# Attention with two feed-forward layers on one core: reads in narrower array tiles, and a new order of steps around the layernorm

## The chip, the cores and the metric

The kernel runs on one core of one Trainium2 chip. The metric is the device time of one execution in microseconds, given as the median of the runs.

## The reference, cut to what matters

```python
# x: [8 batches, 8 heads, 512 tokens, 64], state: [8, 8, 32 states, 64], float32
a  = softmax(x @ state.T / 8)          # each token over the 32 states
xread = a @ state                      # what a token reads from the states
a2 = softmax(state @ x.T / 8)          # each state over the 512 tokens
sread = a2 @ x                         # what a state reads from the tokens
x = concat(xread, sread)               # [8, 544, 512], heads side by side
xn = (x - mean) / sqrt(var + 1e-6) * g_ln
x = x + relu(xn @ w_ch1) @ w_ch2       # hidden width 2048
h = relu(x @ w_in); conv = 3-tap convolution of h along the tokens
out = (h * sigmoid(conv)) @ w_out
```

Everything is float32. Most products are split into a high and a low part and done as three faster products (high by high, low by high, high by low), the lines 633 to 635.

## The kernel before, in words

The first feed-forward layer goes in **units**: unit u is the 512 tokens of batch u, and a tail unit takes the 256 state rows of all batches together. They run in the order 1 to 6, tail, 7; unit 0 is part of the start. A unit has 16 hidden chunks m. `L1` makes a chunk (six matmuls of 512 columns), `L2` adds it to four accumulators (twelve). In `L1` the weights are not multiplied with the tokens: `z_tiles` first multiplies the states of the batch with the weights ("Z"), and `L1` multiplies Z with the softmax weights of the tokens (the tiles `AH`, `AL`).

TensorE takes its instructions in program order. Between its products, in a **gap** before and one after each `L2`, the loop at the end of the program calls `gap(m)`, which issues either a Z product (`z_step`) or the next step of a generator, `tasks`. A `yield` is thus a place where one `L1` or one `L2` goes between two steps. The tasks of unit u are `token_norm(u)`, the layernorm factor of its own tokens, and then `attend(u + 1)`, the attention of the next batch for two groups of four heads, g = 0 and 1. In unit 6 `attend(7)` and `tail_norm` follow, and that unit has an additional gap wherever m is not a multiple of three.

`lnorm` sums over the four chunks on VectorE, splits the sum, and sums over the partitions with a matmul with ones (`mean`, line 494); the second such mean gives the variance. `inv_std` makes the factor: Ln and Exp on ScalarE (lines 532 and 533), then four operations on VectorE. `attn` transposes the tokens on VectorE (`xT`, line 383), and then has these steps: `scores` (line 287), `state_weights` (the states' softmax), `token_weights_1`, `state_weights_t` (transposes on TensorE, line 304, copied by ScalarE, line 306), `token_weights_2`, `state_read` (line 314) with `state_scale` and `token_weights_3`, `state_store` (line 339), `token_read` (line 375). The tiles bP, bQ, bR, bU and bV have one buffer each, so that a writer waits for the last reader.

In `token_read` a state tile `s[:, 2 * g + ql]` holds two heads' states in 64 of its 128 rows, and zeros in the others. In `state_read` each product makes 64 states by two heads, of which `state_scale` keeps the half that belongs together:

```python
T.matmul(sr[64 * ql : 64 * ql + 64, :P], E2T[:, ck, 64 * ql : 64 * ql + 64],
         xn4[:, 2 * ql : 2 * ql + 2, ck, :], start=ck == 0, stop=ck == 3)
```

The start, up to some 150 us, is ordered by the string `START`, in which each letter calls the next step of a stream: T is `attend(1)`, P the products of unit 0, b a step of the weights' conversion on VectorE and GpSimd.

Of the kernel before, what the change touches and what calls it, by code (L numbers as in the profile page):

```python
# [42 lines left out]
def kernel(  # L43
# [223 lines left out]
    def prep_state(b):  # L267
        V.transpose(new_sbd(b).rearrange("p q m -> p (q m)"), s_in.rearrange("p q h r -> p (q h r)"))
        state_parts(b)
# [39 lines left out]
    def state_read(b, g, E2T):  # L309
        sr = bank()  # L310
        xn4 = xnt[b, g]
        for ck in range(4):
            for ql in range(2):
                T.matmul(
                    sr[64 * ql : 64 * ql + 64, :P],
                    E2T[:, ck, 64 * ql : 64 * ql + 64],
                    xn4[:, 2 * ql : 2 * ql + 2, ck, :],
                    start=ck == 0,
                    stop=ck == 3,
                )  # L320
        return sr

    def state_scale(g, sr, z2, B):
# [7 lines left out]
            sr[:, :P].rearrange("p (a d) -> p a d", a=2),  # L331
# [37 lines left out]
    def token_read(b, g):  # L369
# [9 lines left out]
    def attn(b, g):  # L379

        B = work
        xT = new(B["Q"], [2, S])
        V.transpose(flat(xT), xin[b, g])
        if (b, g) not in xnt:
            load_xnat(b, g, new("bP", [1024]))
        yield
        yield
        if g == 0:
            yield
        sc = banks["held"] = scores(b, g, xT)  # L390
# [4 lines left out]
        V.transpose(flat(sT), sc)  # L395
        banks["held"] = None
        yield
# [3 lines left out]
        yield  # L401
        aT = new(B["R"], [S])
        token_weights_2(sT, m1, aT)
# [7 lines left out]
        token_weights_3(aT, b, g, slice(0, S))  # L411
        yield
        state_store(b, g, srz)
        yield
        token_read(b, g)
# [59 lines left out]
    def lnorm(X, t, n, B, add, y):  # L475
# [51 lines left out]
        inv_std(mean(), y, new(B["V"], [n]))  # L527
        banks["held"] = None

    def inv_std(var, y, w):  # L530

        A.activation(w, var, AF.Ln, bias=eps)
        A.activation(y, w, AF.Exp, scale=-0.5)
        V.tensor_tensor(w, y, y, op=ALU.mult)
# [3 lines left out]

    def tail_norm_end():

        y = rstd[NB].unsqueeze(1).to_broadcast([P, KC, TAIL])
        t = new("AH0", [KC, TAIL])
        V.tensor_tensor(t, tns[NB], y, op=ALU.mult)
        tns[NB] = t
# [6 lines left out]
    def attend(u):  # L551
        new_xt(u)
        new_parts(u)
        prep_state(u)
# [4 lines left out]
    def token_norm(u):  # L559
        rstd[u] = new(f"rs{u % 2}", [S])  # L560
        yield from lnorm(XT[u], new("tn", [KC, S]), S, work, V, rstd[u])

    def tail_norm():

        tns[NB] = new("tn", [KC, TAIL])
        rstd[NB] = new("bU", [TAIL])
        yield from lnorm(XTt, tns[NB], TAIL, work, V, rstd[NB])
# [598 lines left out]
```

## Time and profile before

| | us |
|---|---|
| median of 3 runs | 1155.05 (1153.73 to 1155.33) |
| profiled execution, its own time | 1156.01 |
| its span, first to last instruction | 1154.2 |
| TensorE busy | 1120.0 |
| VectorE busy | 720.0 |
| ScalarE busy | 440.9 |
| GpSimd busy | 181.7 |

The profile names tiles without their numbers: `pat` are the two PSUM banks of the tasks, `ph` and `acc` those of `L1` and `L2`. A float32 product that is not split shows as two matmul instructions. A matmul's duration in the profile contains the time to fill and empty the array; the distance between two starts is what it costs in a row of them.

### The profile page before, as it was taken

To read this page: it belongs to the slowest core of one execution; us is meant where nothing else is said; L and a number is where in the kernel's file an instruction comes from. 1 tells how busy PE (TensorE), PEld (TensorE's weight loads), DVE (VectorE), ACT (ScalarE), POOL (GpSimd) and SP (SyncE) were. 2 spreads that over 40 slices of the span, in tenths; PEclk is the share of its full clock that TensorE was granted. 3 is DMA by queue.
4 is the path that set the end of the run, shared out by engine and by line. 5 is a ranking of instruction groups with operands and counts; after the bars stand their busy time and mean duration, and the time that the engine had idled before them with its cause. 6 is when DMAs were issued, how large, how long until landed. Compare 5 with 4: busy or idle time off the path is not lost. (4 is left out here: it accounts for less than half of the span.)

```text
span 1154.2 us, 14521 instructions
## 1 busy us (share of the span) xinstructions
PE 1120.0 (97%) x5393; PEld 847.0 (73%) x5393; DVE 720.0 (62%) x1134; ACT 440.9 (38%) x788; POOL 181.7 (16%) x298
## 2 busy tenths in 40 slices
PE   6999999999999999999999999999999999999997
PEld 5544457777777777777767898788788888888885
DVE  5888666665475565664665723577677666666663
ACT  4565334332333233233333212465344334334342
POOL 2433200000000000000000000265433312212210
PEclk7999999999999999999989999999999999999999
DMA  8565262342333233323323124322112102100001
GB/s 283 159 203 165 60 237 91 80 126 72 76 113 93 68 119 110 96 62 103 97 71 94 70 77 164 110 74 92 37 55 73 37 37 82 38 37 37 1 37 45
DMA packets 129282, 106.29 MB, mean 92 GB/s; under 512 B 103332, under 2 KB 107452, under 8 KB 128188
## 3 DMA queue, kind: packets, MB, share of 16 engines
q1 hardware_dynamic: 129212, 105.37, 29.2%
q8 instruction: 42, 0.69, 0.2%
q14 instruction: 28, 0.23, 0.1%
HBM read 83.85 MB, written 21.50 MB: 91 GB/s over the span
## 5 line engine op out<-in xcount | busy, mean ns | idle before, releaser
L653 DVE SCALAR_TENSOR_TENSOR hL<-ph,hH 128x512 fp32r<-128x512 f32 (+1 forms) x128 | 83.4, 655 | 169.9 <-ACT hH L652 169.7
L633 PE MATMUL acc<-hH,w 128*128 128x512 f32 (+1 forms) x480 | 188.2, 392 | 0.0
L635 PE MATMUL acc<-hH,w 128*128 128x512 f32 (+1 forms) x480 | 181.0, 377 | 0.0
L634 PE MATMUL acc<-hL,w 128*128 128x512 f32 (+1 forms) x480 | 180.6, 376 | 0.0
L652 ACT ACTIVATE hH<-ph 128x512 fp32r<-128x512 f32 (+1 forms) x128 | 72.6, 567 | 193.0 <-PE ph L635 155.5
L1079 DVE SCALAR_TENSOR_TENSOR w<-w,cw,w 128x544 f32<-128x544 f32 x128 | 109.8, 859 | 33.4 <-POOL w L1077 31.6
L633 PEld LDWEIGHTS acc<-hH,w 128*128 128x128 f32 x480 | 90.3, 188 | 43.9 <-issue 16.1
L633 PE MATMUL ph<-AH,ZH 128*128 128x512 f32 x256 | 106.3, 415 | 1.5 <-ACT ZH L608 1.5
L635 PEld LDWEIGHTS acc<-hH,w 128*128 128x128 f32 x480 | 90.2, 188 | 17.3
L634 PEld LDWEIGHTS acc<-hL,w 128*128 128x128 f32 x480 | 90.4, 188 | 16.0 <-DVE hL L653 0.3
L635 PE MATMUL ph<-AH,ZL 128*128 128x512 f32 x256 | 100.9, 394 | 0.0
L634 PE MATMUL ph<-AL,ZH 128*128 128x512 f32 x256 | 100.4, 392 | 0.0
L1060 ACT ACTIVATE w<-w 128x544 f32<-128x544 f32 x64 | 42.1, 658 | 142.1 <-DVE w L1079 142.1
L221 POOL TENSOR_TENSOR ctmp<-ctmp,AH 128x512 int32<-128x512 int32 x1 | 1.3, 1300 | 586.4 <-DVE ctmp L220 586.4
L1067 DVE TENSOR_TENSOR w<-w,w 128x512 fp32r<-128x512 f32 x64 | 50.0, 781 | 42.9 <-ACT w L1066 42.2
L1061 DVE TENSOR_TENSOR w<-w,w 128x544 f32<-128x544 f32 x64 | 48.6, 759 | 40.7 <-ACT w L1060 40.7
L633 PEld LDWEIGHTS ph<-AH,ZH 128*128 128x128 f32 x256 | 48.5, 189 | 22.3 <-issue 8.8
L1066 ACT ACTIVATE w<-w 128x512 fp32r<-128x512 f32 x64 | 40.4, 632 | 51.9 <-DVE w L1061 49.7
L635 PEld LDWEIGHTS ph<-AH,ZL 128*128 128x128 f32 x256 | 48.3, 189 | 12.4 <-DVE ZL L609 2.0
L1077 POOL TENSOR_SCALAR w<-w,cw 128x544 f32<-128x544 f32 x64 | 47.8, 747 | 50.1 <-ACT w L1073 46.9
L634 PEld LDWEIGHTS ph<-AL,ZH 128*128 128x128 f32 x256 | 48.5, 189 | 9.7 <-issue 1.2
L676 PE MATMUL acc<-hH,w 128*128 128x512 f32 x112 | 50.4, 594 | 0.0
(465 smaller groups left out, 2252.9 us busy)
## 6 DMA issues: line engine op xcount, KB each, us to landing
r<-w1d SPq DMA_DIRECT2D x64, 512.0 KB, 4.8
r<-in_moe_w_ch_dram SPq DMA_DIRECT2D x16, 512.0 KB, 5.7
w<-in_moe_w_ch_dram SPq DMA_DIRECT2D x16, 512.0 KB, 8.4
x2d<-XT SPq DMA_DIRECT2D x8, 1024.0 KB, 4.9
bP<-in_x_dram SPq DMA_DIRECT2D x112, 64.0 KB, 2.3
bP<-in_x_dram SPq DMA_DIRECT2D x28, 256.0 KB, 3.3
out_dram<-w SPq DMA_DIRECT2D x24, 256.0 KB, 2.2
w1d<-r SPq DMA_DIRECT2D x8, 512.0 KB, 4.8
```

The source lines that it names most:

```text
L633: T.matmul(o, lh, rh, start=first, stop=False)
L634: T.matmul(o, lh, rl, start=False, stop=False)
L635: T.matmul(o, ll, rh, start=False, stop=last)
L652: A.activation(h, p, AF.Relu)
L653: V.scalar_tensor_tensor(l, p, 0.0, f32(h), op0=ALU.max, op1=ALU.subtract)
L676: T.matmul(acc[d], whole2[m][:, c], h, start=m == 0, stop=m == M1 - 1)
L1060: A.activation(c, c, AF.Sigmoid)
L1061: V.tensor_tensor(c, c, h[:, 1 : SEQ + 1], op=ALU.mult)
L1066: A.activation(g[:, 0], c[:, :S], AF.Copy)
L1067: V.tensor_tensor(g[:, 1], c[:, :S], f32(g[:, 0]), op=ALU.subtract)
L1077: G.tensor_scalar(c, h[:, 0:SEQ], cw[:, f : f + 1], 0.0, op0=ALU.mult, op1=ALU.add)
L1079: V.scalar_tensor_tensor(c, h[:, k : k + SEQ], cw[:, k * FF + f : k * FF + f + 1], c, op0=ALU.mult, op1=ALU.add,)
```

## The change

`token_read` passes only the 64 rows that hold states, so that the two products of a pair use different halves of the array's rows. `state_read` makes each head's 32 states alone: 32 weight columns and 64 streamed columns, sixteen products in place of eight; `state_scale` reads that narrower result twice. The tokens' and states' transposes of the next batch (`begin`) are issued between ScalarE's part of the layernorm factor and VectorE's, in the step of the second mean, and the second group's (`tokens_in`) with `token_weights_3`. The second mean of units 1 to 7 comes one step later (`late`). `state_read` comes before `token_weights_2`, one step after `state_weights_t`. Unit 6 no longer has its extra gaps; from m = 6 on every other `L2` is cut in two with a gap in between. The tail's `tns` is no longer multiplied with its factor before `L1`: three steps of `tail_norm` stay in unit 6, the others go to the tail unit with the layernorm of batch 7, every second gap, and `residual` multiplies the accumulators.

```diff
+    def tokens_in(b, g):
+        xts[b, g] = new(work["Q"], [2, S])
+        V.transpose(flat(xts[b, g]), xin[b, g])
+        if (b, g) not in xnt:
+            load_xnat(b, g, new("bP", [1024]))
+
+    def begin(b):
+        new_xt(b)
+        new_parts(b)
         V.transpose(new_sbd(b).rearrange("p q m -> p (q m)"), s_in.rearrange("p q h r -> p (q h r)"))
-        state_parts(b)
+        tokens_in(b, 0)
...
             for ql in range(2):
-                T.matmul(
-                    sr[64 * ql : 64 * ql + 64, :P],
-                    E2T[:, ck, 64 * ql : 64 * ql + 64],
-                    xn4[:, 2 * ql : 2 * ql + 2, ck, :],
-                    start=ck == 0,
-                    stop=ck == 3,
-                )
+                for hh in range(2):
+                    r = slice(64 * ql + 32 * (hh ^ g), 64 * ql + 32 * (hh ^ g) + 32)
+                    T.matmul(
+                        sr[r, :D], E2T[:, ck, r], xn4[:, 2 * ql + hh, ck, :],
+                        start=ck == 0, stop=ck == 3,
+                    )
...
-                T.matmul(xr[ql], s[:, 2 * g + ql], a, start=i == 0, stop=i == 2)
+                r = slice(64 * ql, 64 * ql + 64)
+                T.matmul(xr[ql], s[r, 2 * g + ql], a[r], start=i == 0, stop=i == 2)
...
     def attn(b, g):
...
-        xT = new(B["Q"], [2, S])
-        V.transpose(flat(xT), xin[b, g])
-        if (b, g) not in xnt:
-            load_xnat(b, g, new("bP", [1024]))
-        yield
-        yield
-        if g == 0:
-            yield
-        sc = banks["held"] = scores(b, g, xT)
+        yield
+        if b == 1:
+            yield
+            if g == 0:
+                yield
+        sc = banks["held"] = scores(b, g, xts[b, g])
         yield
...
         V.transpose(flat(sT), sc)
+        yield
         banks["held"] = None
-        yield
         token_weights_1(sT, m1)
         yield
         E2T = state_weights_t(E2, B)
-        yield
-        aT = new(B["R"], [S])
-        token_weights_2(sT, m1, aT)
         yield
         sr = state_read(b, g, E2T)
...
         srz = state_scale(g, sr, z2, B)
+        yield
+        state_store(b, g, srz)
+        aT = new(B["R"], [S])
+        token_weights_2(sT, m1, aT)
+        yield
         token_weights_3(aT, b, g, slice(0, S))
-        yield
-        state_store(b, g, srz)
-        yield
+        if g == 0:
+            tokens_in(b, 1)
+        yield
+        if b > 1:
+            yield
         token_read(b, g)
...
-        inv_std(mean(), y, new(B["V"], [n]))
+        if late:
+            yield
+        var, w = mean(), new(B["V"], [n])
+        inv_std_1(var, y, w)
+        if follow is not None:
+            begin(follow)
+        inv_std_2(var, y, w)
...
         if u == NB:
-            tasks = token_norm(LAST)
+            tasks = spaced(chain(tail, token_norm(LAST)))
...
-            tasks = chain(token_norm(u), attend(LAST), tail_norm())
+            tail = tail_norm()
+            tasks = chain(token_norm(u), attend(LAST), (next(tail) for _ in range(3)))
...
-            L2(u, m, n)
+            if follow == NB and m > 4 and m % 2 == 0:
+                L2(u, m, n, (0, 1))
+                gap(m)
+                L2(u, m, n, (2, 3))
+            else:
+                L2(u, m, n)
...
             else:
-                gap(m)
-            if follow == NB and m % 3:
                 gap(m)
```

Three places where the order moves. **TensorE, the second mean of unit 3 and what goes before it**, before the change (`ph` rows are an `L1`, `acc` rows an `L2`, `bQ` is the split sum):

```order
L633 MATMUL ph_96<-AH_260_1930,ZH_296_2378 128x512
L634 MATMUL ph_96<-AL_261_1931,ZH_296_2378 128x512
L635 MATMUL ph_96<-AH_260_1930,ZL_297_2379 128x512
L633 MATMUL ph_96<-AH_260_1930,ZH_296_2378 128x512
L634 MATMUL ph_96<-AL_261_1931,ZH_296_2378 128x512
L635 MATMUL ph_96<-AH_260_1930,ZL_297_2379 128x512
L494 MATMUL pat_98<-bQ_2465,ones_85 128x512 x2
L633 MATMUL acc_91<-hH_1141,w_11_171_1129 128x512
```

and with the change, from the mean on (the twelve `acc` rows of an `L2` stand ahead of it; line 297 is `scores`):

```order
L505 MATMUL pat_98<-bQ_2529,ones_85 128x512 x2
L647 MATMUL ph_95<-AH_260_1986,ZH_296_2442 128x512
L648 MATMUL ph_95<-AL_261_1987,ZH_296_2442 128x512
L649 MATMUL ph_95<-AH_260_1986,ZL_297_2443 128x512
L647 MATMUL ph_95<-AH_260_1986,ZH_296_2442 128x512
L648 MATMUL ph_95<-AL_261_1987,ZH_296_2442 128x512
L649 MATMUL ph_95<-AH_260_1986,ZL_297_2443 128x512
L297 MATMUL pat_97<-bQ_2600,sbd_318_2598 64x512 x2
L647 MATMUL acc_91<-hH_1173,w_12_172_1164 128x512
```

The mean now has one more `L2` ahead of it, and the scores of the next batch follow it after one `L1`; before, an `L2`, an `L1` and another `L2` went between.

**VectorE at the same mean**, before (line 489 finishes the split sum, 534 to 537 are the end of the factor, 268 and 383 the transposes of states and tokens, 653 an `L2` operand):

```order
L489 TENSOR_TENSOR bQ_2465<-rs_300_2400,bQ_2465 128x512
L653 SCALAR_TENSOR_TENSOR hL_78<-ph_96,hH_1141 128x512
L534 TENSOR_TENSOR bV_2516<-rs_300_2400 128x512
L535 SCALAR_TENSOR_TENSOR bV_2516<-pat_98,eps_88,bV_2516 128x512
L536 TENSOR_SCALAR bV_2516<-bV_2516 128x512
L537 TENSOR_TENSOR rs_300_2400<-rs_300_2400,bV_2516 128x512
L268 STREAM_TRANSPOSE sbd_318_2526<-s_in_80 128x256
L279 TENSOR_TENSOR s_L_83<-s_raw_81,s_H_82 128x512
L383 STREAM_TRANSPOSE bQ_2530<-bP_2269 128x1024
```

and with the change (500, 554 to 557, 278 and 271, 667):

```order
L500 TENSOR_TENSOR bQ_2529<-rs_300_2464,bQ_2529 128x512
L667 SCALAR_TENSOR_TENSOR hL_78<-ph_96,hH_1173 128x512
L278 STREAM_TRANSPOSE sbd_318_2598<-s_in_80 128x256
L271 STREAM_TRANSPOSE bQ_2600<-bP_2307 128x1024
L554 TENSOR_TENSOR bV_2592<-rs_300_2464 128x512
L555 SCALAR_TENSOR_TENSOR bV_2592<-pat_98,eps_88,bV_2592 128x512
L556 TENSOR_SCALAR bV_2592<-bV_2592 128x512
L557 TENSOR_TENSOR rs_300_2464<-rs_300_2464,bV_2592 128x512
L289 TENSOR_TENSOR s_L_83<-s_raw_81,s_H_82 128x512
```

The two transposes moved from behind the factor's four operations to ahead of them.

**TensorE in unit 6, group 0, from the transposed state weights to the state read**, before (an `L1` between):

```order
L304 MATMUL pat_98<-ident_84,bR_4331 128x128 x4
L633 MATMUL ph_96<-AH_428_3712,ZH_464_4160 128x512
L634 MATMUL ph_96<-AL_429_3713,ZH_464_4160 128x512
L635 MATMUL ph_96<-AH_428_3712,ZL_465_4161 128x512
L633 MATMUL ph_96<-AH_428_3712,ZH_464_4160 128x512
L634 MATMUL ph_96<-AL_429_3713,ZH_464_4160 128x512
L635 MATMUL ph_96<-AH_428_3712,ZL_465_4161 128x512
L314 MATMUL pat_97<-bP_4268,bV_4367 64x128 x8
```

and with the change (half an `L2` between; `L314` is now the transposes, `L326` the read):

```order
L314 MATMUL pat_98<-ident_84,bR_4463 128x128 x4
L647 MATMUL acc_93<-hH_1173,w_13_192_1340 128x512
L648 MATMUL acc_93<-hL_78,w_13_192_1340 128x512
L649 MATMUL acc_93<-hH_1173,w_13_192_1340 128x512
L647 MATMUL acc_94<-hH_1173,w_13_192_1340 128x512
L648 MATMUL acc_94<-hL_78,w_13_192_1340 128x512
L649 MATMUL acc_94<-hH_1173,w_13_192_1340 128x512
L326 MATMUL pat_97<-bP_4432,bV_4493 32x64 x16
```

Six matmuls stand between the two in both. The read is now sixteen products of 32 weight columns, and the token softmax's second part is no longer issued ahead of it.

## Rows read from the trace of the kernel before

**Rows 1.** The page, engines: busy us, share of the span, instructions.
```profile
PE 1120.0 (97%) x5393; PEld 847.0 (73%) x5393; DVE 720.0 (62%) x1134; ACT 440.9 (38%) x788; POOL 181.7 (16%) x298
```

**Rows 2.** Waits of TensorE, whole span: total us, times, longest us.
```profile
PE pat L494 <- ACT bQ L487: 4.1, 3, 3.2
PE pat L494 <- DVE bQ L489: 2.8, 7, 0.5
PE pat L339 <- DVE bV L329: 1.9, 5, 0.6
```

**Rows 3.** Timeline, TensorE, about a token read, unit 2: start us, us, what.
```profile
313.72 0.39 PE L635 MATMUL acc<-hH,w 128*128 128x512 f32 x1
...
315.53 0.39 PE L634 MATMUL acc<-hL,w_e 128*128 128x512 f32 x1
```

**Rows 4.** Timeline, TensorE, at the second mean, unit 3.
```profile
340.02 0.39 PE L494 MATMUL pat<-bQ,ones 128*128 128x512 f32 x1
340.87 0.50 PE L494 MATMUL pat<-bQ,ones 128*128 128x512 f32 x1 [0.46 <-DVE bQ L489]
...
341.90 0.40 PE L633 MATMUL acc<-hH,w 128*128 128x512 f32 x1
```

**Rows 5.** Timeline, TensorE, at the second mean, unit 6.
```profile
575.84 0.39 PE L635 MATMUL acc<-hH,w 128*128 128x512 f32 x1
579.41 1.52 PE L494 MATMUL pat<-bQ,ones 128*128 128x512 f32 x2 [3.19 <-ACT bQ L487]
...
586.13 0.39 PE L634 MATMUL acc<-hL,w 128*128 128x512 f32 x1
```

**Rows 6.** Windows, TensorE: stretch, length, busy us (instructions), granted clock, DMA.
```profile
579.40:585.70 6.30, 6.29 (x24) 0.50 0.01 3
46.00:50.00 4.00, 2.66 (x24) 1.00 0.00 0
```

**Rows 7.** Timeline, TensorE, last before and second after a Z product.
```profile
320.52 0.39 PE L635 MATMUL ph<-AH,ZL 128*128 128x512 f32 x1
...
322.19 0.39 PE L634 MATMUL acc<-hL,w 128*128 128x512 f32 x1
```

**Rows 8.** Windows of 0.02 us, line 599: matmuls in flight stand as (x).
```profile
320.82:320.84 0.02, 0.01 (x1) 1.00 0.00 0
320.88:320.90 0.02, 0.02 (x8) 1.00 0.33 77
321.32:321.34 0.02, 0.02 (x16) 1.00 0.00 0
```

**Rows 9.** Timeline, TensorE, last before and second after a state read.
```profile
308.26 0.39 PE L635 MATMUL acc<-hH,w 128*128 128x512 f32 x1
...
309.94 0.40 PE L634 MATMUL ph<-AL,ZH 128*128 128x512 f32 x1
```

**Rows 10.** Timeline, TensorE, tail unit, 256-column products and the mean.
```profile
652.74 0.28 PE L633 MATMUL acc<-hH,w 128*128 128x256 f32 x1
652.86 0.28 PE L634 MATMUL acc<-hL,w 128*128 128x256 f32 x1
...
653.82 1.89 PE L666 MATMUL ph<-AH,r 128*128 128x256 f32 x8
...
657.23 0.28 PE L633 MATMUL acc<-hH,w 128*128 128x256 f32 x1
```

**Rows 11.** Timeline, VectorE, after the second mean, unit 3.
```profile
342.79 0.69 DVE L534 TENSOR_TENSOR bV<-rs 128x512 f32<-128x512 f32 x1 [1.25 <-ACT rs L533]
...
346.31 1.24 DVE L383 STREAM_TRANSPOSE bQ<-bP 128x1024 f32<-128x1024 f32 x1
...
352.06 0.68 DVE L296 TENSOR_REDUCE m<-pat 128x1 f32<-128x512 f32 x1
```

**Rows 12.** Timeline, ScalarE, unit 3: softmax exponential, and copy of transposed weights.
```profile
355.97 0.63 ACT L350 ACTIVATE bU<-bU 128x512 f32<-128x512 f32 x1 [2.23 <-DVE bU L349]
...
385.57 0.58 ACT L306 ACTIVATE bV<-pat 128x512 f32<-128x512 f32 x1
```

More of the change, by code (lines that the diff above doesn't have):

```diff
@@ L264, in ensure @@
             return self.done[i]
-    def prep_state(b):
+    xts = {}
+    def tokens_in(b, g):
[6 more added lines that the diff above has]
+        new_parts(b)
         V.transpose(new_sbd(b).rearrange("p q m -> p (q m)"), s_in.rearrange("p q h r -> p (q h r)"))
-        state_parts(b)
+        tokens_in(b, 0)
     sbd = {}
@@ L330, in state_scale @@
             srz,
-            sr[:, :P].rearrange("p (a d) -> p a d", a=2),
+            sr[:, :D].unsqueeze(1).to_broadcast([P, 2, D]),
             rm.unsqueeze(2).to_broadcast([P, 2, D]),
@@ L410, in attn @@
         srz = state_scale(g, sr, z2, B)
-        token_weights_3(aT, b, g, slice(0, S))
         yield
         state_store(b, g, srz)
+        aT = new(B["R"], [S])
+        token_weights_2(sT, m1, aT)
         yield
+        token_weights_3(aT, b, g, slice(0, S))
+        if g == 0:
[3 more added lines that the diff above has]
+            yield
         token_read(b, g)
@@ L472, in tokens_start, with lnorm @@
         token_weights_3(aT, 0, slice(0, 2), HALF[h])
-    def lnorm(X, t, n, B, add, y):
+    def lnorm(X, t, n, B, add, y, late, follow):
         cols = [slice(c, c + 256) for c in range(0, n, 256)]
@@ L526, in lnorm, with inv_std_1, inv_std_2 @@
         yield
-        inv_std(mean(), y, new(B["V"], [n]))
+        if late:
[5 more added lines that the diff above has]
+        inv_std_2(var, y, w)
         banks["held"] = None
-    def inv_std(var, y, w):
+    def inv_std_1(var, y, w):
         A.activation(w, var, AF.Ln, bias=eps)
         A.activation(y, w, AF.Exp, scale=-0.5)
+    def inv_std_2(var, y, w):
         V.tensor_tensor(w, y, y, op=ALU.mult)
@@ L537, in inv_std @@
         V.tensor_tensor(y, y, w, op=ALU.mult)
[L539 to L544, printed above, removed]
     tns, rstd = {}, {}
@@ L551, in attend @@
     def attend(u):
-        new_xt(u)
-        new_parts(u)
-        prep_state(u)
+        if u == 1:
+            begin(u)
+        state_parts(u)
         yield from attn(u, 0)
@@ L560, in token_norm @@
         rstd[u] = new(f"rs{u % 2}", [S])
-        yield from lnorm(XT[u], new("tn", [KC, S]), S, work, V, rstd[u])
+        follow = u + 1 if 0 < u < LAST else None
+        yield from lnorm(XT[u], new("tn", [KC, S]), S, work, V, rstd[u], u > 0, follow)
     def tail_norm():
-        tns[NB] = new("tn", [KC, TAIL])
+        tns[NB] = new("v0", [KC, TAIL])
         rstd[NB] = new("bU", [TAIL])
-        yield from lnorm(XTt, tns[NB], TAIL, work, V, rstd[NB])
+        yield from lnorm(XTt, tns[NB], TAIL, work, V, rstd[NB], False, None)
     Z, pieces = {}, {}
@@ L669, in L1, with L2 @@
         relu_parts(u, m, p)
-    def L2(u, m, n):
+    def L2(u, m, n, ds=range(KC)):
         h, l = (t[:, :n] for t in hidden(m))
-        for d in range(KC):
+        for d in ds:
             c = slice(P * d, P * d + P)
@@ L688, in residual @@
         if u == NB:
+            t = new("tn", [KC, TAIL])
             for d in range(KC):
-                V.tensor_tensor(XTt[:, d], XTt[:, d], acc[d][:, :n], op=ALU.add)
+                V.tensor_tensor(t[:, d], acc[d][:, :n], rstd[u], op=ALU.mult)
+            V.tensor_tensor(XTt, XTt, t, op=ALU.add)
             return
@@ L960, with spaced @@
     splits = {(1, m): [m + 2] for m in range(SPLITS - 2, M1 - 2)}
+    def spaced(steps):
+        for _ in steps:
+            yield
+            yield
     L1(1, 0)
@@ L1010 @@
                     pass
-                if follow == NB:
-                    tail_norm_end()
-            else:
-                gap(m)
-            if follow == NB and m % 3:
+            else:
                 gap(m)
```

## The prediction

> **What bounds the kernel now.** I read the page first, then the waits of TensorE, then its timeline where it waits. TensorE is busy 97% of the span [rows 1], and what it runs there can't be left out, except for work that is wider than it need be. So two things can make this kernel shorter: fewer array cycles for the same products, and the few waits that TensorE still has. The waits [rows 2] show where: the mean's matmuls waited 4.1 us for ScalarE and 2.8 us for VectorE, and the state store 1.9 us in five places. VectorE and ScalarE are off the path wherever these waits do not stand.
>
> Such a wait costs more than the listed idle time, because a matmul's duration hides the beginning of it. From the last matmul ahead of a token read to the second after it there are eight intervals in 315.53 - 313.72 = 1.81 us [rows 3], so one 512-column matmul costs 0.226 us; an `L1` is 6 x 0.226 = 1.36 us, an `L2` 2.72 us, a token read 1.36 us. It has no cost at its edges.
>
> **Waits that the change takes away.**
>
> (a) The second mean in units 1 to 5. Its first matmul starts at 340.02, the fourth matmul after its second one at 341.90 [rows 4]: 1.88 us for five intervals, where 5 x 0.226 = 1.13 us would do. The wait costs 0.75 us. VectorE ended the sum's low part only then. With one more `L2` (2.72 us) ahead of the mean, the operand is ready. 5 x 0.75 = 3.75 us.
>
> (b) The same place in unit 6, where the additional gaps put the steps closer together. From the last ordinary matmul at 575.84 to 586.13 [rows 5] 10.29 us pass. Between these are two means, six `L1` matmuls, a Z product and the intervals around them. What a Z product costs: from the last matmul before it to the second after it 322.19 - 320.52 = 1.67 us [rows 7], less two intervals 1.22 us. So 10 x 0.226 + 1.22 = 3.48 us would do, and the loss is 6.8 us. Half of it is not the wait: after it the granted clock was 0.50, the lower of the two levels (1.2 GHz), for 6.3 us [rows 6]. A wait of 1.3 us elsewhere left the clock at 1.00 (the second row of [rows 6]). With the gaps of the other units at this place the wait goes: 6.8 us.
>
> (c) The first mean in the tail unit: eight `L1` matmuls end at 653.82 + 1.89 = 655.71, two means at 0.226 each should be followed by an `L2` at 656.16, and it came at 657.23 [rows 10]. 1.1 us, gone since the steps are now two gaps apart.
>
> (d) The last state store of unit 6 waited because read and store had nothing between them. Of the 1.9 us [rows 2] I take 0.4 us for it; now an `L2` is between.
>
> **Work that the change makes narrower.** Both reads occur in 14 places in batches 1 to 7.
>
> (e) State read. Before: 309.94 - 308.26 = 1.68 us [rows 9], less two intervals 1.23 us. How much of that is streaming? The Z product shows it: eight tiles of the array start within 0.06 us of each other, and all eight second passes have begun 0.44 us later [rows 8]. One pass of 512 float32 columns costs 0.43 us, with eight tiles side by side. The Z product streams two passes, 0.86 us, and 0.36 us is the change of tile shape and back. The state read streams 16 passes of 128 columns, two at a time: 8 x 0.107 = 0.86 us, the rest is 0.37 us. After: 32 passes of 64 columns, four at a time: 8 x 0.054 = 0.43 us, and the same 0.37 us. That is a gain of 0.43 us if the tiles run side by side, nothing if each start costs 0.027 us (32 of them are 0.86 us), and a loss of 32 x 0.054 - 0.86 = 0.87 us if they run one after the other. I take 0.43 us, since the Z product's eight starts took 0.06 us and have the same 32 weight columns. 14 x 0.43 = 6.0 us.
>
> The Trainium skill speaks against this step: "TensorEngine Tiling (Array Packing)", section "Performance Considerations", puts a floor of about 60 cycles under every matmul and advises against tiling a dimension that is already small. The starts of the Z product are closer than that floor, so the trace does not bear it out for matmuls in different tiles. By that rule the state read would gain nothing, and the sum would be smaller by 6.0 us.
>
> (f) Token read. Six matmuls become three pairs, each pair in two halves of the rows, and the change of tile shape, 0.36 us, is new here. A pair streams as long as one matmul, 0.226 us, but needs two weight loads of 128 columns. Matmuls of 256 columns with such a load each start 0.12 us apart [rows 10], so two loads may take 0.24 us. I take the 0.24: 3 x 0.24 + 0.36 = 1.08 us, a gain of 0.28 us. At best it is 1.36 - 3 x 0.213 - 0.36 = 0.36 us, at worst, with no overlap, a loss of 0.36 us. 14 x 0.28 = 3.9 us.
>
> **Waits that the change adds.** Let t be the start of the second mean.
>
> (g) Scores. The token transpose writes bQ, which the mean still reads, so VectorE starts it when the mean is done. The mean's two matmuls start at t and t + 0.23 and end about 0.39 us after that; with some delay the transpose starts at t + 0.66, takes 1.24 us [rows 11], and ends at t + 1.9. TensorE comes to the scores after 0.45 + 1.36 + 0.09 = 1.90 us. They meet; I charge 0.1 us, six times: 0.6 us. Behind the transposes wait the factor's four operations, but these waited for ScalarE's Exp anyway (1.25 us) [rows 11], which the transposes now fill.
>
> (h) State read in unit 6, group 0. The read stands half an `L2` behind the weights' transposes. ScalarE copies these only after the tokens' exponential, which is the end of a long chain. The factor's first operation began 1.92 us after the second mean matmul (340.87 to 342.79), and the scores' maximum can now begin when the factor, the low part of the states and an `L2` operand are through: t + 0.2 + 1.9 + 2.6 + 0.6 + 0.6 = t + 5.9. From that maximum to the exponential 355.97 - 352.06 = 3.9 us passed [rows 11, 12], and an `L2` operand of 0.6 us now comes between: t + 10.4. Exponential and copy are 0.55 and 0.6 us [rows 12]: t + 11.55. TensorE arrives after the mean, an `L1`, the scores, one and a half `L2` and `L1`, the transposes and half an `L2`: 0.45 + 1.36 + 1.3 + 2.72 + 1.36 + 1.36 + 0.45 + 1.36 = t + 10.35. It waits 1.2 us, once. In units 1 to 5 a Z product comes at t + 11.7 and needs the bank that this copy empties: just free.
>
> **Moved at no cost.** `token_weights_2` and the second group's transposes are later on VectorE, and an `L2` operand waits behind them; there is an additional `L1` and `L2` ahead of the token read, so the operand is needed some 2 us after it is ready. The input loads on SP's queue keep their order; group 1's load still starts at the state read, and its transpose two gaps later. In the start the state store now follows the read directly and waits for `state_scale`, about 0.5 us twice, in place of waits of the same kind [rows 2]; the narrower reads of batch 0 run into later waits for the weights' conversion. I take 0 there, between a loss of 1.5 and a gain of 2.5 us. The tail's product with its factor, now on the accumulators, is behind two `L1`.
>
> **The sum.** 3.75 + 6.8 + 1.1 + 0.4 + 6.0 + 3.9 = 21.95 us gained, 0.6 + 1.2 = 1.8 us lost: 20.2 us. The profiled execution took 1156.0 us, 0.96 above the median; it would take 1135.8, and the median goes from 1155.05 to 1134.9 us.
>
> **Rivals.**
>
> A. The state read gains nothing, as every start has its price: 1134.9 + 6.0 = 1140.9. For it: no row shows 32 passes as short as 64 columns. Against it: the starts of the Z product. 18%. (The rule of the Trainium skill weighed at (e) would give this case.)
>
> B. The wait of (h) is longer than worked out and brings the clock down, as in (b): 6.8 in place of 1.2 us, 1140.5. The row at 1.3 us says no, but my chain has many links. 10%.
>
> C. The start gains too, and the reads reach their best: 2.5 us there, 14 x 0.08 = 1.1 us more: some 1131.5. 17%.
>
> D. The second mean is late again, as VectorE falls behind by as much as TensorE gains: 3.75 us not gained, 1138.7. 5%.
>
> E. The other side: the narrow tiles do not run side by side, in row halves or for short passes. Then a token read costs 0.36 us more and a state read 0.87 us more than before: 14 x (0.64 + 1.30) = 27.2 us worse than forecast, 1162.1. It decides once the two reads together lose 20.2 / 14 = 1.44 of these 1.94 us. Z's rows speak against it. 3%.
>
> My own case has 47%.
>
> **How the numbers follow.** The range of 1128 to 1144 us leaves out E, and the cases in which A and B come together or C is larger than worked out. About 0.2% (2.3 us) is what a measurement of this kernel can tell from no change. All cases but E are faster by more than that: faster 0.95, same 0.02, slower 0.03.
>
> **What would show it.** Right: the waits of the mean for VectorE and ScalarE all but gone after 150 us; a granted clock of 1.00 through unit 6; a state read of about 0.8 us and a token read of 1.08 us between ordinary matmuls; one wait of about 1.2 us of the state read for the copy in unit 6. Wrong: reads as long as before or longer, a second stretch at the lower clock, or a wait at the scores or the Z product in every unit.

## The result and the profile after

| | before | after |
|---|---|---|
| median, us | 1155.33 (1153.73 to 1155.85) | 1136.29 (1135.14 to 1137.6) |
| ratio after to before, 95% interval | | 0.984 (0.9829 to 0.9851) |
| span of the profiled execution, us | 1154.2 | 1134.5 |
| TensorE busy, us | 1120.0 | 1104.2 |
| mean granted clock, share of full speed | 0.987 | 0.990 |

The change makes the kernel 1.6% faster. 1134.9 us were forecast, 1.4 us below the measured median. Taken from one median to the other, 20.2 us of gain were forecast and 19.0 came.

The page, engines, of the kernel after (busy us, share of the span, instructions), which answers to [rows 1]:

```profile
PE 1104.2 (97%) x5649; PEld 830.3 (73%) x5649; DVE 720.4 (63%) x1134; ACT 438.2 (39%) x788; POOL 181.5 (16%) x298
```

TensorE has 256 instructions more and is busy 15.8 us less; VectorE does the same work as before. Of the 19.7 us by which the span is shorter, the other 3.9 us are idle time.

TensorE's waits, whole span, after (total us, times, longest us), which answer to [rows 2]:

```profile
PE pat L481 <- DVE bU L475: 3.3, 1, 3.3
PE ph L647 <- ACT w L1096: 2.9, 2, 1.5
PE pat L348 <- DVE w L338: 2.2, 1, 2.2
PE pat L348 <- DVE bV L338: 2.1, 2, 1.6
...
PE pat L635 <- POOL r L221: 1.2, 2, 0.7
...
PE pat L326 <- ACT bV L316: 0.9, 1, 0.9
...
PE pat L314 <- DVE ZL L623: 0.6, 1, 0.6
PE pat L505 <- DVE bQ L500: 0.6, 1, 0.6
```

The mean (now line 505) waited 6.9 us in ten places; one wait of 0.6 us is left, in the tail unit. Between 147 and 560 us no wait of a task is left but one of 0.7 us at a Z product. The first two rows lie in the start and after the tail and have their counterparts before. New are the read's wait for ScalarE's copy (line 316) in unit 6, which was forecast, a wait of the transposes (line 314) there, which was not, and in the start 1.65 us of a state store (line 348; 0.62 before) and a second wait of 0.47 us for GpSimd (line 635, a product that makes a mean of the weights while they are converted).

**Where the time went, by units.** The first `residual` instruction on VectorE marks the end of a unit. This table is worked out from the starts of these instructions in the two timelines (us between marks; the forecast is worked out from the terms of the prediction, 2 x 0.43 + 2 x 0.28 + 0.75 - 0.1 = 2.07 us for an ordinary unit). Batch 1's second token read starts at 150.40 us before and 150.53 after, behind the first mark, so it counts for unit 1:

| | before | after | gain | forecast |
|---|---|---|---|---|
| start, to the end of unit 0 | 148.43 | 148.07 | 0.36 | 1.14 (2 x 0.43 + 0.28) |
| unit 1 | 86.85 | 84.23 | 2.62 | 2.35 (2.07 + 0.28) |
| units 2 to 5, each | 80.90 to 80.94 | 78.80 to 78.85 | 2.05 to 2.10 | 2.07 |
| unit 6 | 87.95 | 80.93 | 7.02 | 7.3 |
| tail and unit 7 | 127.02 | 125.63 | 1.39 | 1.1 |
| the rest | 380.31 | 380.32 | 0.0 | 0 |

The four ordinary units came out within 0.03 us of the forecast. The start and unit 6 stayed below it, unit 1 and the tail came out above.

TensorE at the second mean of unit 3, after, which answers to [rows 4] (start us, duration us, instruction):

```profile
337.69 0.62 PE L505 MATMUL pat<-bQ,ones 128*128 128x512 f32 x2
338.14 0.39 PE L647 MATMUL ph<-AH,ZH 128*128 128x512 f32 x1
```

The mean costs 338.14 - 337.69 = 0.45 us, as two ordinary matmuls do. Its wait is gone.

TensorE about a state read and a token read of unit 2, after, which answer to [rows 9] and [rows 3]:

```profile
299.78 0.39 PE L649 MATMUL acc<-hH,w 128*128 128x512 f32 x1
300.10 0.65 PE L326 MATMUL pat<-bP,bV 128*32 128x64 f32 x32
300.69 0.50 PE L647 MATMUL ph<-AH,ZH 128*128 128x512 f32 x1
301.02 0.40 PE L648 MATMUL ph<-AL,ZH 128*128 128x512 f32 x1
...
308.89 0.39 PE L649 MATMUL acc<-hH,w 128*128 128x512 f32 x1
309.21 0.50 PE L385 MATMUL pat<-AH,s_H 64*128 64x512 f32 x2
...
310.10 0.50 PE L647 MATMUL acc<-hH,w_e 128*128 128x512 f32 x1
310.44 0.40 PE L648 MATMUL acc<-hL,w_e 128*128 128x512 f32 x1
```

Read as in the prediction, from the last ordinary matmul to the second one after it less two intervals: the state read costs 301.02 - 299.78 - 0.45 = 0.79 us (before 1.23), the token read 310.44 - 308.89 - 0.45 = 1.10 us (before 1.36).

TensorE in unit 6, windows, after (stretch, length, busy us of the engines, granted clock, DMA), which answers to [rows 6], and the two waits there in the timeline:

```profile
560.00:640.00 80.00, 78.49 (x451) 58.96 (x450) 47.44 (x85) 25.32 (x45) 0.00 (x0) 1.00 0.25 73
```

```profile
585.60 0.65 PE L326 MATMUL pat<-bP,bV 128*32 128x64 f32 x32 [0.87 <-ACT bV L316]
...
608.44 0.66 PE L314 MATMUL pat<-ident,bR 128*128 128x128 f32 x4 [0.64 <-DVE ZL L623]
```

The granted clock is 1.00, the level of 2.4 GHz, through the unit; before it was 0.50 (1.2 GHz) for 6.3 us behind the wait of 3.19 us [rows 5, 6]. Two waits of 0.87 and 0.64 us did not bring it down.

### The profile page after: what moved, and what is told of

The parts are those of the page before. It is cut to its first block, busy times and chain, and to the rows that moved or that the text cites. A ratio compares the mean times of both kernels' runs of the same rounds, so it can differ in the third digit from the quotient of the medians.

```text
span 1134.5 us, 14987 instructions
## 1 busy us (share of the span) xinstructions
PE 1104.2 (97%) x5649; PEld 830.3 (73%) x5649; DVE 720.4 (63%) x1134; ACT 438.2 (39%) x788; POOL 181.5 (16%) x298
```

## Experiments

The theory: the gain is a sum of separate things, the narrower reads, the second mean without its wait, and unit 6 without its tight spacing, and each is worth its term. The rivals: the reads gain nothing by being narrow and the new order alone brings the gain; or the reads' gain needs the new order to get through; and for unit 6, that a wait taken away there comes back at its end. Where experiments are compared, "per unit" means units 2 to 5 between the marks of the table above.

**1. Each read twice.** Every product of both reads is issued twice, the second time over the first, which prices them by themselves.

```diff
-        for ck in range(4):
+        for ck in (0, 1, 2, 3, 0, 1, 2, 3):
...
-            for i, (s, a) in enumerate(((s_H, h), (s_L, h), (s_H, l))):
+            for i, (s, a) in [*enumerate(((s_H, h), (s_L, h), (s_H, l)))] * 2:
```

> The changed kernel with the products of every token read and state read issued twice (the second pass starts the sums anew, so the values stay). It measures what the narrow products cost without their edges. If the tiles run side by side, the state read grows by 8 x 0.054 = 0.43 us and the token read by 3 x 0.23 = 0.68 us in each of the 12 places of units 1 to 6: a unit of 78.83 us becomes 78.83 + 2 x 1.11 = 81.05 us. If every start of a short pass has a price of 0.027 us, the state read grows by 0.86 us and the unit to 81.9 us. If nothing overlaps, by 1.7 and 1.36 us, and the unit to 84.9 us.

1149.38 us (one run). TensorE at the same two reads of that kernel, timeline:

```profile
302.69 0.39 PE L649 MATMUL acc<-hH,w 128*128 128x512 f32 x1
303.01 1.10 PE L326 MATMUL pat<-bP,bV 128*32 128x64 f32 x64
...
304.38 0.40 PE L648 MATMUL ph<-AL,ZH 128*128 128x512 f32 x1
...
312.25 0.39 PE L649 MATMUL acc<-hH,w 128*128 128x512 f32 x1
...
314.49 0.40 PE L648 MATMUL acc<-hL,w_e 128*128 128x512 f32 x1
```

The state read becomes 304.38 - 302.69 - 0.45 = 1.24 us, 0.45 more than the single one. So 32 passes of 64 columns cost 0.45 us, 0.014 us each, where 0.43 was worked out for four side by side, and 0.79 - 0.45 = 0.34 us are left, which the prediction put down to the change of tile shape and back. The token read becomes 314.49 - 312.25 - 0.45 = 1.79 us: 0.69 more for three pairs, 0.23 us for a pair of row halves. That is the price of one full matmul, so two weight loads fit beside one pass.

**2. and 3. The change with one wide read.** Each gives one read back its former form.

```diff
-                r = slice(64 * ql, 64 * ql + 64)
-                T.matmul(xr[ql], s[r, 2 * g + ql], a[r], start=i == 0, stop=i == 2)
+                T.matmul(xr[ql], s[:, 2 * g + ql], a, start=i == 0, stop=i == 2)
```

> The changed kernel with the token read undone: all 128 rows again. By the forecast's working a token read goes back from 1.10 to 1.36 us and loses its edges; units 2 to 5 grow by 2 x 0.26 = 0.52 us each, and over 14 places the kernel by some 3.6 us, to about 1139.9 us. Rival: a wide read has no change of tile shape, and its matmuls only fill what the reads' followers wait for; then the units stay within 0.1 us of 78.83 us and the time within 0.5 us of 1136.3 us.

```diff
-                for hh in range(2):
-                    r = slice(64 * ql + 32 * (hh ^ g), 64 * ql + 32 * (hh ^ g) + 32)
-                    T.matmul(sr[r, :D], E2T[:, ck, r], xn4[:, 2 * ql + hh, ck, :], ...)
+                T.matmul(sr[64 * ql : 64 * ql + 64, :P], E2T[:, ck, 64 * ql : 64 * ql + 64],
+                         xn4[:, 2 * ql : 2 * ql + 2, ck, :], ...)
... (and state_scale as before)
```

> The changed kernel with the state read undone: 64 weight columns and 128 streamed columns again. By the forecast's working a state read goes back from 0.79 to 1.23 us: units 2 to 5 grow by 0.88 us each, the kernel by some 5 to 6 us, to about 1142 us. Rival: short passes have a price at each start and the gain of the units comes from elsewhere; then the units stay within 0.1 us of 78.83 us.

The wide token read: 1139.6 us (1139.02 to 1140.86), ratio 0.9869 (0.9854 to 0.9883). The wide state read: 1140.43 us (1139.81 to 1141.53), ratio 0.9875 (0.9861 to 0.989). Per unit they cost some 0.46 to 0.51 and 0.88 to 0.91 us more than the change, two reads of each: about 0.24 and 0.45 us a read, where 1.36 - 1.10 = 0.26 and 1.23 - 0.79 = 0.44 say the same within 0.02 us. So in the units of the new order each read's gain arrives nearly in full. In the start it does not: from the scores of batch 1 to the first mark the kernel with the wide token read takes 67.75 us, the change 67.74. The whole kernel with the wide state read came out below the 1142 us expected; its profile has the first mark at 146.41 us, 1.66 us earlier than the change, and the start differs between executions (last section).

**4. The narrow reads in the kernel before.** Both reads narrow, the old order.

```diff
# in the kernel before
+                r = slice(64 * ql, 64 * ql + 64)
+                T.matmul(xr[ql], s[r, 2 * g + ql], a[r], start=i == 0, stop=i == 2)
...
+                for hh in range(2):
+                    r = slice(64 * ql + 32 * (hh ^ g), 64 * ql + 32 * (hh ^ g) + 32)
+                    T.matmul(sr[r, :D], E2T[:, ck, r], xn4[:, 2 * ql + hh, ck, :], ...)
... (and state_scale for the narrower result)
```

> The kernel before with both reads made narrow and its order kept. By the forecast's working units 2 to 5 fall from 80.91 by 2 x (0.44 + 0.26) = 1.40 us to 79.5 us; unit 6 keeps its loss at the second mean (4.87 us for a block that costs 0.46 us elsewhere) and the lower clock after it; in all some 9 us less, about 1146.5 us. The start gives back most of what it gains, as in the changed kernel, so 8 us is the lower end. Rival: the narrower reads only let TensorE come earlier to the waits of the second mean, which grow by as much; then the units stay near 80.9 us.

1151.15 us (1147.47 to 1152.29), ratio 0.9956 (0.9942 to 0.9969). The reads cost 0.79 and 1.10 us as in the change, 2 x 0.70 = 1.40 us per unit less than before, but the units are shorter by 0.67 to 0.70 us only: half of what was expected. TensorE's waits for VectorE at the state store, whole span, of this kernel, and the store in unit 2:

```profile
PE pat L338 <- DVE bV L328: 3.7, 5, 1.0
```

```profile
309.42 0.39 PE L635 MATMUL ph<-AH,ZL 128*128 128x512 f32 x1
309.90 0.33 PE L338 MATMUL pat<-ident,bV 128*128 128x128 f32 x1
309.99 0.48 PE L633 MATMUL acc<-hH,w 128*128 128x512 f32 x1
```

The store stands one `L1` behind the read, and VectorE's scaling of it came too late. VectorE in the same stretch:

```profile
307.44 0.69 DVE L355 TENSOR_TENSOR bU<-bU,m 128x512 f32<-128x512 f32 x1
308.24 0.71 DVE L356 STREAM_TRANSPOSE bR<-bU 128x512 f32<-128x512 f32 x1
...
309.55 0.29 DVE L328 TENSOR_TENSOR bV<-pat,rm 128x128 f32<-128x128 f32 x1
```

The second part of the tokens' softmax (lines 355 and 356) holds VectorE to 308.95 us, and the scaling (line 328) ends at 309.84. When the read ends earlier, the store only waits longer: it costs 0.43 us in place of 0.12. The gain is the read's to make and the order's to pass on.

**5. The same, with the read ahead of the tokens' softmax.**

```diff
# in the kernel of 4
         E2T = state_weights_t(E2, B)
         yield
-        aT = new(B["R"], [S])
-        token_weights_2(sT, m1, aT)
-        yield
         sr = state_read(b, g, E2T)
...
         srz = state_scale(g, sr, z2, B)
+        yield
+        state_store(b, g, srz)
+        aT = new(B["R"], [S])
+        token_weights_2(sT, m1, aT)
+        yield
         token_weights_3(aT, b, g, slice(0, S))
         yield
-        state_store(b, g, srz)
-        yield
         token_read(b, g)
```

> The kernel before with both reads narrow and, of the new order, only this: the state read one step after the transposed weights, ahead of the second part of the tokens' softmax, and the state store ahead of that part too. With the narrow reads alone a unit fell by 0.7 us, as the state store's block grew from 0.12 to 0.43 us. Theory: the store waits for VectorE's scale, which stands behind the softmax's second part; with the read ahead of it the store's block goes back to 0.12 us and units 2 to 5 fall to 80.91 - 1.40 = 79.5 us. Rival: the store's block grows because the read now ends earlier than any VectorE order could follow; then it stays at 0.4 us and the units at 80.2 us. A wait of the read for ScalarE's copy of the weights, one L1 earlier than before, would show as a read above 0.79 us.

1149.94 us (1147.62 to 1151.3), ratio 0.9957 (0.994 to 0.9974). Per unit it gains 1.30 to 1.34 us on the kernel before, twice as much as in 4 and nearly all of the 1.40. As a whole it gains no more than 4 (ratio 0.9956), because unit 6, with its tight spacing, lost 1.85 us on the kernel before: a token read waited there 2.21 us for ScalarE.

```profile
624.34 0.50 PE L375 MATMUL pat<-AH,s_H 64*128 64x512 f32 x2 [2.21 <-ACT AH L365]
```

So moving the state read, with its scaling and store, ahead of the softmax's second part lets the narrow reads through, and with unit 6 spaced as before it loses there what the other units gain.

**6. Unit 6 alone: no extra gaps at the second mean.**

```diff
# in the kernel before
-            if follow == NB and m % 3:
+            if follow == NB and m % 3 and m > 5:
```

> The kernel before with the extra gaps of unit 6 only from m = 7 on, so that its layernorm and the first group's attention run at the pace of the other units. By the forecast's working the second mean there waits 0.75 us as in units 1 to 5 in place of 4.4 us, the granted clock stays at 1.00, and unit 6 falls from 87.95 by about 6 us to 82 us. The tail's factor now ends one L2 before the tail's first product, which may wait for it: up to 3 us back in the tail, so 1149 to 1152 us in all. Rival: the loss in unit 6 comes from its being the one whose tasks hold the tail's layernorm as well, not from the pace; then unit 6 stays above 86 us and the lower clock shows up in another place.

1157.08 us (1154.92 to 1158.33), ratio 1.0023 (1.0014 to 1.0032): slower by 0.2%, though the stretch did what (b) says. Unit 6 takes 90.11 us in place of 87.95.

```profile
570.00:590.00 20.00, 19.54 (x97) 14.92 (x96) 13.58 (x21) 8.16 (x13) 0.00 (x0) 1.00 0.27 100
```

The clock is 1.00, the second mean costs 1.19 us in place of 4.87, the Z product 1.22 in place of 2.81. The time came back at the end of the unit. TensorE's waits from 630 to 670 us of that kernel:

```profile
PE pat L494 <- ACT bQ L487: 1.9, 3, 1.1
PE acc L634 <- DVE hL L653: 1.5, 1, 1.5
PE ph L666 <- DVE AH L543: 1.4, 1, 1.4
```

With fewer gaps the attention ends later, and the whole of `tail_norm` falls behind it, where `L1` of the tail needs its product (line 543) at once.

**7. The same, with the tail's factor out of unit 6**, as in the change: multiplied into the accumulators, its steps two gaps apart.

```diff
# in the kernel of 6
...
+            t = new("tn", [KC, TAIL])
             for d in range(KC):
-                V.tensor_tensor(XTt[:, d], XTt[:, d], acc[d][:, :n], op=ALU.add)
+                V.tensor_tensor(t[:, d], acc[d][:, :n], rstd[u], op=ALU.mult)
+            V.tensor_tensor(XTt, XTt, t, op=ALU.add)
...
-            tasks = token_norm(LAST)
+            tasks = spaced(chain(tail, token_norm(LAST)))
...
-            tasks = chain(token_norm(u), attend(LAST), tail_norm())
+            tail = tail_norm()
+            tasks = chain(token_norm(u), attend(LAST), (next(tail) for _ in range(3)))
...
-                if follow == NB:
-                    tail_norm_end()
```

> The kernel before with the extra gaps of unit 6 only from m = 7 on, and with the tail's layernorm split as in the change: three steps in unit 6, the rest in the tail unit at every second gap, the factor multiplied onto the accumulators. Theory: slower gaps alone gained nothing because the tail's layernorm then waits at the end of unit 6; with it moved away, the second mean of unit 6 waits 0.75 us, nothing waits at the end, and from the residual of unit 5 to the tail's first product it takes 89.8 - 6 = 83.8 us; the tail saves another 1.1 us: about 1148 us. Rival: unit 6 simply has too many steps for its gaps whoever holds the tail; then waits of some us remain at its end and the time stays above 1152 us.

1150.75 us (1149.17 to 1152.3), ratio 0.9968 (0.9958 to 0.9978). Between the marks, unit 6 takes 84.70 us (before 87.95) and the tail and unit 7 125.62 (before 127.02): 4.65 us gained together, where 6 lost. In the change the same parts gained 8.4 us; of the rest 1.40 us is the reads and 0.73 the later mean. In this kernel the last Z product of unit 6 (2.43 us), the last state store (1.14) and the first mean of the tail (1.12) still stall; in the change they cost 1.22, 0.12 and 0.24 us. That the half `L2`s make this difference, and not the order of the other steps, no run shows by itself; with one half `L2` fewer (11) the Z product and the mean stall again.

**8. The mean without its extra step.**

```diff
-        if late:
-            yield
```

> The changed kernel without the additional step ahead of the second mean. By the forecast's working that mean waits again for the low part of the split sum: its block costs 1.19 us in place of 0.46 us, six times, while the scores lose their 0.05 us; units 2 to 5 grow by 0.7 us to 79.5 us, the kernel by 4 us to about 1140.3 us. Rival: VectorE reaches the low part earlier in the changed kernel because its attention steps lie elsewhere; then the mean does not wait and the units stay at 78.83 us.

1140.42 us (1139.04 to 1140.72), ratio 0.9878 (0.9861 to 0.9894). The second mean of unit 3 in this kernel:

```profile
334.30 0.39 PE L505 MATMUL pat<-bQ,ones 128*128 128x512 f32 x1
335.15 0.50 PE L505 MATMUL pat<-bQ,ones 128*128 128x512 f32 x1 [0.46 <-DVE bQ L500]
335.49 0.39 PE L645 MATMUL acc<-hH,w 128*128 128x512 f32 x1
```

It is the row of before [rows 4], with the same wait of 0.46 us, and a mean costs 1.19 us again. Per unit 0.77 to 0.84 us are lost. The rest of the change does not remove the wait; it takes the extra step.

**9. The transposes behind the factor, with the rest of the change.**

```diff
         inv_std_1(var, y, w)
-        if follow is not None:
-            begin(follow)
         inv_std_2(var, y, w)
+        if follow is not None:
+            begin(follow)
```

> The changed kernel with the two transposes behind VectorE's four operations of the factor, as before, but with the scores still one L1 behind the mean. By the forecast's working the token transpose ends at t + 6.3 in place of t + 1.9, so the scores wait 4.4 us in each of the units 1 to 6, which is longer than the 3.2 us after which the clock went down in unit 6 of the kernel before; with the lower clock behind each wait a unit grows by 4.4 to 8 us, the kernel by 26 to 48 us, to 1162 to 1184 us. Rival: the order on VectorE is of no account, as it is idle a third of the time; then 1136 us.

1173.39 us (one run). The scores are now so close behind the mean that the transposes have to be first. TensorE's waits, whole span, and VectorE behind the second mean of unit 3, which TensorE issued at 349.33 us:

```profile
PE pat L297 <- DVE bQ L271: 25.7, 6, 4.4
```

```profile
351.37 0.69 DVE L554 TENSOR_TENSOR bV<-rs 128x512 f32<-128x512 f32 x1 [3.24 <-ACT rs L550]
...
353.95 0.44 DVE L278 STREAM_TRANSPOSE sbd<-s_in 128x256 f32<-128x256 f32 x1
354.31 1.20 DVE L271 STREAM_TRANSPOSE bQ<-bP 128x1024 f32<-128x1024 f32 x1
```

VectorE waits for ScalarE and then does the factor, with both transposes in line behind. Six scores blocks cost 5.8 to 6.8 us in place of 1.26. The factor begins 351.37 - 349.33 = 2.04 us after the mean. In the change, with both transposes ahead of it, it begins 339.73 - 337.69 = 2.04 us after the mean too: they fill the time for which it waits anyway, and the scores there cost 0.05 us more than elsewhere.

**10. The state store of the start, one step later.** In batch 1 alone, the store goes behind the tokens' softmax and a step further.

```diff
         yield
-        state_store(b, g, srz)
+        if b > 1:
+            state_store(b, g, srz)
         aT = new(B["R"], [S])
         token_weights_2(sT, m1, aT)
         yield
+        if b == 1:
+            state_store(b, g, srz)
```

> The changed kernel with the state store of batch 1, in the start, one step later, so that products stand between read and store as before. In the changed kernel the store waits there 1.65 and 0.47 us for VectorE. Theory: the start is bound by the weights' conversion on VectorE and GpSimd; then these waits go, those for GpSimd's converted weights (0.74 and 0.47 us at the means of the weights) grow, and the time stays within 0.4 us of 1136.3 us. Rival: the waits at the store are what ate the batch 1 gain of the start (1.4 us expected, 0.4 us seen); then some 1 us less, about 1135.3 us.

1135.03 us (1133.94 to 1136.31), ratio 0.9831 (0.9816 to 0.9846), the fastest here; its interval overlaps that of the change, so the stretch itself has to decide. TensorE behind the first state read of batch 1, after and in this kernel, and for this kernel also the mean of the weights that follows the second scores (line 638):

```profile
96.82 0.65 PE L326 MATMUL pat<-bP,bV 128*32 128x64 f32 x32
99.12 0.33 PE L348 MATMUL pat<-ident,bV 128*128 128x128 f32 x1 [1.65 <-DVE bV L338]
99.29 3.60 PE L690 MATMUL acc<-hH,w 128*128 128x512 f32 x8
```

```profile
96.25 0.65 PE L326 MATMUL pat<-bP,bV 128*32 128x64 f32 x32
96.83 3.70 PE L693 MATMUL acc<-hH,w 128*128 128x512 f32 x8
...
101.76 0.27 PE L348 MATMUL pat<-ident,bV 128*128 128x128 f32 x1
...
113.81 2.74 PE L638 MATMUL pat<-r,gmean 128*128 128x512 f32 x6
117.53 1.13 PE L638 MATMUL pat<-r,gmean 128*128 128x512 f32 x2 [0.99 <-POOL r L221]
118.50 3.60 PE L693 MATMUL acc<-hH,w 128*128 128x512 f32 x8
```

From the scores of batch 1 to the end of unit 0 it took 67.53 us before (67.55 and 67.54 in 6 and 7, which leave the start as it was), 67.74 us after (67.74 in 8, which leaves the change's start), and 66.09 us here. That is 1.65 us less than the change, repeated in 11 (66.11 us), and 1.44 us less than before.

The reads make 1.14 us of the 1.44, two state reads and one token read (2 x 0.44 + 0.26); the second token read stands behind the mark. The rest is a balance. By the distances between starts the two stores cost some 1.8 us before, 2.5 after and 0.2 here. The mean of the weights behind the second scores takes 119.95 - 116.52 = 3.43 us to the next product before, without a wait, 120.23 - 116.06 = 4.17 after, and 118.50 - 113.81 = 4.69 here, as it waits for GpSimd. So both sides of the expectation were partly right: the stores' stall did eat gain, and the wait for the converted weights did grow when the stall went.

What makes the first store so late, GpSimd and VectorE in the kernel after:

```profile
97.33 1.29 POOL L221 TENSOR_TENSOR w<-ctmp,w 128x512 int32<-128x512 int32 x1 [5.67 <-issue]
```

```profile
97.49 1.15 DVE L336 TENSOR_SCALAR rm<-hmask,z 128x2 f32<-128x2 f32 x1
```

Line 336, a part of `state_scale`, works on two columns and takes 0.23 us in the units. Here it takes 1.15 us and ends 0.02 us behind GpSimd's operation on the weights. In the traces of before, after and this kernel it takes 1.15 to 1.28 us in the seven places where such an operation runs beside it, and ends with it each time. By an estimate from these durations, 1.15 - 0.23, some 0.9 of the 1.65 us of waiting are this meeting; that the one operation holds the other is read from the times, and no run moves them apart.

**11. The same, and unit 6's half `L2`s from m = 8 on.**

```diff
# in the kernel of 10
-            if follow == NB and m > 4 and m % 2 == 0:
+            if follow == NB and m > 6 and m % 2 == 0:
```

> The changed kernel with two edits: the state store of batch 1 one step later (as measured alone), and the cut of an L2 with a gap in unit 6 from m = 8 on in place of 6. The second puts a whole L2 and L1 more between the second mean and the state read: its block, 1.74 us in the changed kernel, should come down to 0.79 us, and unit 6 from 80.93 to about 80 us. With the 1.3 to 1.7 us of the start: about 1134 us. Rival: with two gaps fewer the tail's first steps come too late in unit 6 and wait there; then unit 6 stays at 80.9 us or above.

1137.27 us (1136.82 to 1138.21), ratio 0.9855 (0.984 to 0.987): a miss. The start repeats 10 (66.11 us), and the read's wait for the copy in unit 6 is gone, but unit 6 takes 83.82 us, 2.89 more than in the change. TensorE's waits in its timeline, in unit 6:

```profile
595.27 0.50 PE L385 MATMUL pat<-AH,s_H 64*128 64x512 f32 x2 [0.68 <-ACT AH L375]
...
619.73 0.50 PE L385 MATMUL pat<-AH,s_H 64*128 64x512 f32 x2 [0.68 <-ACT AH L375]
```

The edit takes one gap away (m = 6), not two as the expectation says. With a gap fewer each later step comes sooner behind its predecessor: two token reads wait for the softmax weights and cost 2.11 us each in place of 1.10, and the last Z product costs 2.42 us. The 0.95 us that the wait of (h) costs is the cheaper place for it.

## Why the prediction was right

- **(a), the second mean in units 1 to 5.** Right in cause and size: 1.19 us became 0.46, 0.73 of the 0.75 us forecast; experiment 8 puts it back.
- **(b) and (d), unit 6.** The sizes were right: unit 6 gained 7.02 of some 7.3 us, and the clock stayed at 1.00. Block by block (b) came to 6.75 us (4.41 at the mean, 1.60 at the Z product, 0.74 in ordinary matmuls at the lower clock) and (d) to 0.41. The prediction's reason was incomplete. It said that with the other units' gaps the wait goes; the wait does, but experiment 6 shows that this alone gains nothing, as the stall reappears at the tail's layernorm. The gain is shared by three parts of the change: the fewer gaps, the tail's factor moved out (7), and, for what 7 leaves, the half `L2`s, which no run takes out by themselves. The row by which the prediction expected the clock to stay up after 1.3 us of waiting [rows 6] ends with that wait; the same trace has 1.00 from 50 to 60 us too.
- **(c)** gained 1.39 us with unit 7, where 1.1 was forecast.
- **(e) and (f), the reads.** Sizes: 0.44 and 0.26 us a read against 0.43 and 0.28. The short passes do run side by side (1). Rivals A and E fall by experiments 1 to 3, and with A the rule that was weighed at (e): the Trainium skill, "TensorEngine Tiling (Array Packing)", section "Performance Considerations", would have the state read gain nothing, and 0.014 us for a pass in experiment 1 is shorter than that page's floor of about 60 cycles (0.025 us at 2.4 GHz, an estimate from the page's figure). In row halves the upper bound that I took for a pair, 0.24 us for two loads, is 0.23 us. What the prediction did not price is that (e) needs the moved read: in the old order half is lost (4), in the new one it is not (5).
- **(g)** came to 0.05 us instead of 0.1, each time: the meeting of transposes and scores was worked out rightly, and 9 shows what it is worth.
- **(h)** came to 0.95 us instead of 1.2, and the clock stayed up: rival B falls. Beside it a cost came that the prediction had not: the second group's transposes in unit 6 cost 1.32 in place of 0.45 us, waiting for a Z product's low part on VectorE. That unit 6 still came within 0.3 us is in part luck: (h) was smaller than priced, and the second mean of the tail, 0.32 us, left the unit.
- **The step that failed** is in "Moved at no cost": that the store behind the read in the start waits about 0.5 us twice "in place of waits of the same kind", so that the start stands at 0 beside a full count of 14 places for (e) and (f). From the scores of batch 1 to the first mark these places should have given 1.14 us; 0.21 us was lost (67.53 to 67.74). The stores waited 1.65 and 0.47 us, where they had waited 0.62 and 0.49, which cost some 0.7 us more, and a mean of the weights that had not waited before waited 0.47 us for GpSimd and took 0.74 us more. The loss of 1.35 us against the count lies within the 1.5 us that the prediction allowed. Experiment 10 takes the stores' wait away and brings more than this back. The moment at which batch 1's scores begin differs by itself between executions, from 78.3 to 81.8 us in these kernels; that it came at 80.90 before and at 80.33 after can't be counted for the change.
- **Unit 1** gained 2.62 us where its terms make 2.35 with the token read of batch 1 that falls into it. Its two state stores, which the sum left out, cost 0.59 and 0.53 us before and 0.12 and 0.27 after, and one block of transposes 0.72 before and 0.45 after; a Z product that costs 1.91 us in place of 1.22 takes 0.69 of that back, and a state read at 0.85 us another 0.06. That makes 2.60 us.
- Rival C (start and reads at their best) did not come: it needs 2.5 us from the start beside the reads' count, and even in 10 the start gave 1.44 us where the count is 1.14. Rival D did not occur.

## What to carry to other kernels

A narrower product gains only if what uses its result can follow: look at what stands ahead of that consumer on its engine, and move the product and the consumer together. A wait taken away in a dense stretch is worth its price only when the steps that it delays have slack at the end of that stretch. When a move is applied to all iterations, price it anew in the start and in the last one, where the same engine has other work in its queue.

## What was not expected of the hardware

- 32 passes of 64 float32 columns, each with 32 weight columns, in four column tiles cost 0.45 us together. What is left of the blocks, 0.34 us for the state read and 1.10 - 0.69 = 0.41 us for the token read's row halves, appears with the narrow tiles (a wide token read costs six ordinary matmuls and no more, 1.36 us) and is nearly as much as the products of the state read themselves.
- A VectorE operation on two columns took 0.23 us by itself and 1.15 to 1.28 us beside a GpSimd operation, and ended with it (10).
- The start differs from execution to execution even where the program is the same there: in the kernels after, 8 and 9 the first scores of batch 1 come at 80.33, 78.57 and 81.04 us, and the granted clock from 8 to 16 us is 0.65, 1.00 and 0.73. What sets it was not tried.
